# ScalarE forms two small attention operands in the first two token tiles, and small attention tiles get six buffers

## The chip, the cores and the metric

The kernel runs on one core of a Trainium2 chip. Five engines work side by side: TensorE (PE; its weight loads are PEld), VectorE (DVE), ScalarE (ACT), GpSimd (POOL) and SyncE (SP), which here only issues DMAs. The metric is the device time of one execution in microseconds, lower is better. Before the change the median of three runs is 1221.68 us (1221.15 to 1223.91).

## The reference

Three stages follow each other. Attention has 2 batches, 8 heads, 576 positions and head size 64, and keeps only the 32 largest scores of each row:

```
kth = np.partition(scores, -top_k, axis=-1)[..., -top_k:-top_k + 1]
scores = np.where(scores >= kth, scores, -1e9)
attn = np.exp(scores - np.max(scores, axis=-1, keepdims=True))
attn = attn / (np.sum(attn, axis=-1, keepdims=True) + 1e-09)
```

Its 1152 x 512 result goes through a mixture of 8 dense experts (ReLU, 512 to 1024 to 512), whose outputs are weighted by a gate that eight rounds of row and column normalisation over all tokens make. A last feed-forward layer (512 to 2048 to 512, Mish) follows.

## The kernel before, in words

The 1152 tokens form nine tiles of 128 rows, and the tiles form three chunks: tiles 0 and 1, tiles 2 and 3, tiles 4 to 8 (CHUNKS). A unit is one tile and one head (t, h). Each unit goes through five steps: scores (PE, then an eviction to SBUF by ScalarE, L235), threshold (L246 to L265), mask (L275 to L291), norm (L294 to L306) and values (transposes at L325, products with V at L348 and L355).

The threshold is VectorE's: four MAX8 instructions find eight maxima each (L254), and three MATCH_REPLACE8 strike out what was found (L261); each reads 576 columns, so a unit takes seven such passes. The first maximum, times -0.125, is the bias `nb` of the exponential (L271). The last of the 32 maxima is the threshold of the mask.

The first 13 units (POOL_UNITS; all of tile 0 and heads 0 to 4 of tile 1) are "on_pool": VectorE writes a mask of 0 or a large negative number (L285), GpSimd adds the scores (L286), and ScalarE takes the exponential and with it the row sum `sm` (L272). The other units take the exponential first and let VectorE mask and sum it (L290). In norm, `r` is the row sum plus epsilon (L299), then its reciprocal (L300), both on VectorE, and ScalarE scales the row by it (L305).

When tile 1 is done, the experts start on chunk 0. An expert is cut into eight pieces of 128 hidden columns. For a piece PE forms h (12 matmuls, L619), ScalarE rounds it to hh (L537), VectorE forms the rest hl (L538), and two pieces later PE forms y (L596). h has two PSUM buffers, so the h of piece k+2 can only start when hl of piece k has been read. The remaining attention (tiles 2 to 8) is woven between the pieces.

PE's order is written out by the program. On the other engines a scheduler sets the order, by priorities (the streams `first`, `evict`, `prep`, `attn`, `moe`, `fill`, in that order) and by when an operand would be there by its own reckoning. One rule is fixed by hand: the first MAX8 of each unit of tile 2 stands behind the last reciprocal of tile 1 (`ends`). Scores of tiles 2, 3 and parts of 5 and 6 are computed early, into tiles `early`, `early_xh`, `early_xl`.

Of the kernel before, what the change touches and what calls it, by code (L numbers as in the profile page):

```python
# [10 lines left out]
F32 = mybir.dt.float32  # L11
F32R = mybir.dt.float32r
U32 = mybir.dt.uint32
AF = mybir.ActivationFunctionType
ALU = mybir.AluOpType
# [4 lines left out]
P = 128  # L20
B, H, S, D = 2, 8, 576, 64
# [13 lines left out]
TOPK = 32  # L35
NEG = -3.0e38
SCALE = 0.125
EPS = 1e-9
TINY2 = ((1 + 1 / 16) * 2.0**-15) ** 2

CHUNKS = [(0, 1), (2, 3), (4, 5, 6, 7, 8)]
# [32 lines left out]
def attention_moe_moe2(ctx: ExitStack, tc: tile.TileContext, qT, kT, vm, vt, wg, wst, w64, out):  # L74
    nc = tc.nc
# [5 lines left out]
    def after(inst, earlier):  # L81

        tc.add_manual_dep(
            inst.ins,
            earlier.ins.name,
            mybir.DependencyInfo(mybir.DependencyClass.NoSync, mybir.DependencyReason.DATA),
            reason="order",
        )

    def pool(name, bufs=1, space=None, stack=ctx, side="left", **kw):  # L90
        if space is not None:
            kw["space"] = space
        return stack.enter_context(tc.tile_pool(name=name, bufs=bufs, side=side, **kw))

    const = pool("const")
    small = pool("small", 4)
# [13 lines left out]
    sp = pool("sp", 2, stack=att)  # L110
# [35 lines left out]
    qset, live, away = {}, {}, {}  # L146
# [98 lines left out]
    def threshold(t, h, on_pool):  # L245

        with st("attn"):
            s = live["s", t, h]
            top = small.tile([P, TOPK], F32, tag="top", name=f"top_{t}_{h}")
            w = sp.tile([P, S], F32, tag="w", name=f"w_{t}_{h}")  # L250
            src = s
            for i in range(TOPK // 8):
                g = top[:, 8 * i : 8 * i + 8]
                top8 = nc.vector.max(g, src)  # L254
                if i == 0 and t == CHUNKS[0][-1] + 1:
                    if "ends" in live:
                        after(top8, live["ends"])
                    else:
                        live.setdefault("held", []).append(top8)
                if i + 1 < TOPK // 8:  # L260
                    nc.vector.match_replace(w, g, src, NEG)  # L261
                    src = w
            live["top", t, h] = top
            if not on_pool:
                live["e", t, h] = exponential(t, h, sp.tile([P, S], F32, tag="e", name=f"e_{t}_{h}"), s, nc.vector)  # L265
        yield from ()

    def exponential(t, h, dst, src, eng, **kw):

        nb = small.tile([P, 1], F32, tag="nb", name=f"nb_{t}_{h}")  # L270
        eng.tensor_scalar(nb, live["top", t, h][:, 0:1], -SCALE, None, op0=ALU.mult)  # L271
        nc.scalar.activation(dst, src, AF.Exp, bias=nb, scale=SCALE, **kw)  # L272
        return dst

    def mask(t, h, on_pool):  # L275

        with st("attn"):
            s = live.pop(("s", t, h))
            sm = small.tile([P, 1], F32, tag="sm", name=f"sm_{t}_{h}")
            kth = live["top", t, h][:, TOPK - 1 : TOPK]  # L280
            if h % 2 == 0:
                live["pair", t, h] = sp.tile([P, 2 * S], F32, tag="em", name=f"em_{t}_{h}", bufs=3)
            em = live["pair", t, h - h % 2][:, h % 2 * S :][:, :S]
            if on_pool:
                nc.vector.tensor_scalar(em, s, kth, NEG, op0=ALU.is_lt, op1=ALU.mult)  # L285
                nc.gpsimd.tensor_tensor(em, em, s, ALU.add)  # L286
                exponential(t, h, em, em, nc.vector, accum_out=sm)
            else:
                e = live.pop(("e", t, h))
                nc.vector.scalar_tensor_tensor(em, s, kth, e, op0=ALU.is_ge, op1=ALU.mult, accum_out=sm)  # L290
            live["em", t, h], live["sm", t, h] = em, sm  # L291
        yield from ()

    def norm(t, h, on_pool):  # L294
        with st("attn"):
            em, sm = live["em", t, h], live.pop(("sm", t, h))
            r = small.tile([P, 1], F32, tag="r", name=f"r_{t}_{h}")
            with st("moe" if on_pool else "attn"):
                nc.vector.tensor_scalar(r, sm, EPS, None, op0=ALU.add)  # L299
                inv = nc.vector.reciprocal(r, r)  # L300
            if (t, h) == (CHUNKS[0][-1], H - 1):
                live["ends"] = inv
                for inst in live.pop("held", ()):
                    after(inst, inv)
            nc.scalar.activation(em, em, AF.Copy, scale=r)  # L305
        yield from ()  # L306
# [96 lines left out]
    def attention():  # L403
# [10 lines left out]
        for u, (t, h) in enumerate(units):  # L414
            pooled = u < POOL_UNITS
            for order, (stage, delay) in enumerate(
                (
                    (scores, 0),
                    (partial(threshold, on_pool=pooled), AHEAD),
                    (partial(mask, on_pool=pooled), AHEAD + 1),  # L420
                    (partial(norm, on_pool=pooled), AHEAD + (2 if pooled else 1)),
                    (values, AHEAD + (3 if pooled else 2)),
                )
            ):
                plan.setdefault(u + delay, []).append((order, u, partial(stage, t, h)))
# [434 lines left out]
```

## Time and profile before

| | |
|---|---|
| median of three runs | 1221.68 us |
| profiled execution | 1221.39 us, its span 1219.6 us |
| PE busy | 1168.7 us, 96% of the span |
| VectorE busy | 854.7 us, 70% |
| ScalarE busy | 660.2 us, 54% |
| GpSimd busy | 540.8 us, 44% |
| chain that ended last | PE 86%, DVE 11% |

Shares over the whole span hide the stages. Read them by stretch: where PE is below full there is something it waits for, and the engine that is full there sets the pace. Starts are in us from the start of the span. In a timeline the second number is the time that the row took, and an engine's next instruction can start before the last has ended; the distance from start to start is what an instruction costs its engine.

### The profile page before, as it was taken

The page shows a single profiled execution, that of the slowest core. Times are in us where ns is not written, and L with a number is a line of the kernel's source. Part 1 is how long each engine was busy: PE and PEld are TensorE (multiplying, and loading weights), DVE is VectorE, ACT ScalarE, POOL GpSimd, SP SyncE. Part 2 cuts the span into 40 slices and gives each one's busy share as a digit, 9 for nine tenths or more (in the row PEclk, how much of TensorE's full clock was granted, in tenths as well). Part 3 has the DMA queues.
Part 4 walks back from the last instruction along what each step waited for, and adds up shares of the span by engine and source line. Part 5 has one row for each costly group of instructions (what it writes and reads, how often), then busy time and mean ns, then how long its engine had stood idle before and what let it go on. Part 6 is the DMA issues. An engine that isn't in the chain of part 4 may idle for free.

```text
span 1219.6 us, 21194 instructions
## 1 busy us (share of the span) xinstructions
PE 1168.7 (96%) x7459; PEld 1048.4 (86%) x7459; DVE 854.7 (70%) x1873; ACT 660.2 (54%) x1321; POOL 540.8 (44%) x424
## 2 busy tenths in 40 slices
PE   2677999999999999999999999999999999999998
PEld 2566888998989899899999999999999999999997
DVE  7999999999999999713656868677666633433221
ACT  6786777877777778654223333333333334554432
POOL 7844778877777877774112112121121122221210
PEclk9899999999999999999999999999999999999999
DMA  8434565576655555665235665656445332223201
GB/s 258 126 129 152 171 178 170 170 224 188 211 163 168 157 162 164 186 220 169 70 89 180 199 190 176 207 178 192 138 134 160 119 98 64 93 95 114 78 26 44
DMA packets 105114, 183.20 MB, mean 150 GB/s; under 512 B 14128, under 2 KB 24624, under 8 KB 105008
## 3 DMA queue, kind: packets, MB, share of 16 engines
q1 hardware_dynamic: 103712, 180.68, 47.6%
q8 instruction: 58, 0.95, 0.3%
q10 hardware_dynamic: 1296, 1.18, 0.3%
q14 instruction: 48, 0.39, 0.1%
HBM read 158.55 MB, written 23.27 MB: 149 GB/s over the span
## 4 chain that ended last, share of the span: by engine, by line
PE 86%; DVE 11%; DMA 1%; ACT 1%; issue 0%; POOL 0%; SPq 0%; POOLq 0%; ACTq 0%
PE h_c2e L619 18%; PE y_c2e L596 18%; PE h_d L619 8%; PE y_d L596 8%; PE y_c0e L596 7%; PE h_c0e L619 7%; PE h_c1e L619 6%; PE y_c1e L596 6%; DVE top L254 4%; DVE w L261 4%; PE pv L348 2%; PE tr L325 2%; PE sc L226 2%; PE pv L355 1%; DVE em L290 1%; DMA wraw_c0e<-in_wst_dram 1%
## 5 line engine op out<-in xcount | busy, mean ns | idle before, releaser
L522 POOL TENSOR_TENSOR wl_c2e<-wraw_c2e,wh_c2e 128x512 fp32r<-128x512 f32 x64 | 84.2, 1315 | 341.2 <-ACT wh_c2e L520 326.5
L522 POOL TENSOR_TENSOR wl_c0e<-wraw_c0e,wh_c0e 128x512 fp32r<-128x512 f32 x128 | 171.6, 1356 | 53.1 <-ACT wh_c0e L520 50.9
L522 POOL TENSOR_TENSOR wl_c1e<-wraw_c1e,wh_c1e 128x512 fp32r<-128x512 f32 x128 | 173.3, 1371 | 48.6 <-ACT wh_c1e L520 45.2
L520 ACT ACTIVATE wh_c2e<-wraw_c2e 128x512 fp32r<-128x512 f32 x128 | 80.8, 632 | 186.9 <-PE y_c2e L596 95.0
L254 DVE MAX8 top<-w 128x8 f32<-128x576 f32 x216 | 157.8, 747 | 0.8
L619 PE MATMUL h_c2e<-xh,wh_c2e 128*128 128x256 f32 (+1 forms) x512 | 158.3, 309 | 0.0
L619 PE MATMUL h_c2e<-xl,wh_c2e 128*128 128x256 f32 (+1 forms) x512 | 158.0, 309 | 0.0
L619 PE MATMUL h_c2e<-xh,wl_c2e 128*128 128x256 f32 (+1 forms) x512 | 157.8, 308 | 0.0
L538 DVE SCALAR_TENSOR_TENSOR hl_c2e<-h_c2e,hh_c2e 128x256 fp32r<-128x256 f32 (+1 forms) x128 | 62.5, 488 | 99.7 <-ACT hh_c2e L537 99.3
L596 PE MATMUL y_c2e<-wh_c2e,hh_c2e 128*128 128x512 f32 x320 | 126.0, 394 | 0.0
L596 PE MATMUL y_c2e<-wl_c2e,hh_c2e 128*128 128x512 f32 x320 | 125.9, 394 | 0.0
L596 PE MATMUL y_c2e<-wh_c2e,hl_c2e 128*128 128x512 f32 x320 | 125.2, 391 | 0.0
L522 POOL TENSOR_TENSOR wl_d<-wraw_d,wh_d 128x512 fp32r<-128x512 f32 x32 | 41.5, 1297 | 160.2 <-ACT wh_d L520 160.2
L520 ACT ACTIVATE wh_c0e<-wraw_c0e 128x512 fp32r<-128x512 f32 x128 | 80.5, 629 | 52.9 <-PE y_c0e L596 21.0
L261 DVE MATCH_REPLACE8 w<-top,w 128x576 f32<-128x576 f32 x144 | 106.4, 740 | 0.0
L557 DVE TENSOR_TENSOR hl_d<-mg_d,hh_d 128x256 fp32r<-128x256 f32 x64 | 38.5, 602 | 91.7 <-ACT hh_d L556 91.7
L520 ACT ACTIVATE wh_c1e<-wraw_c1e 128x512 fp32r<-128x512 f32 x128 | 80.3, 629 | 40.4 <-PE y_c1e L596 16.4
L619 PEld LDWEIGHTS h_c2e<-xh,wh_c2e 128*128 128x128 f32 x512 | 96.2, 188 | 2.5
L619 PEld LDWEIGHTS h_c2e<-xl,wh_c2e 128*128 128x128 f32 x512 | 96.1, 188 | 2.3
L619 PEld LDWEIGHTS h_c2e<-xh,wl_c2e 128*128 128x128 f32 x512 | 96.8, 189 | 0.0
L226 PE MATMUL sc<-ks,q 128*128 128x288 f32 x320 | 63.1, 330 | 26.0 <-ACT early L239 8.2
L537 ACT ACTIVATE hh_c2e<-h_c2e 128x256 fp32r<-128x256 f32 (+1 forms) x128 | 54.8, 428 | 55.3 <-PE h_c2e L619 53.0
(170 smaller groups left out, 3352.8 us busy)
## 6 DMA issues: line engine op xcount, KB each, us to landing
wraw_c0e<-in_wst_dram SPq DMA_DIRECT2D x128, 256.0 KB, 3.0
wraw_c1e<-in_wst_dram SPq DMA_DIRECT2D x128, 256.0 KB, 3.0
wraw_c2e<-in_wst_dram SPq DMA_DIRECT2D x128, 256.0 KB, 3.0
cx<-in_w_dram SPq DMA_DIRECT2D x32, 512.0 KB, 4.2
wraw_d<-w SPq DMA_DIRECT2D x64, 256.0 KB, 2.6
yd<-ysp SPq DMA_DIRECT2D x32, 256.0 KB, 3.6
yb<-yd SPq DMA_DIRECT2D x32, 256.0 KB, 3.2
w<-cc SPq DMA_DIRECT2D x32, 256.0 KB, 3.5
```

The lines of the kernel that those rows point to most:

```text
L226: nc.tensor.matmul(halves[half], q[:, h % HG, :], ks[b, h][:, half * HS : (half + 1) * HS], start=(i == 0), stop=(i == len(terms) - 1),)
L254: top8 = nc.vector.max(g, src)
L261: nc.vector.match_replace(w, g, src, NEG)
L325: nc.tensor.transpose(tr[:, c, :], em[:, j * D + c * P :][:, :P], ident)
L348: nc.tensor.matmul(pv[i * D : (i + 1) * D, pair, c0:c1], vmain[b, pair][:, i, c, :], live["at", i][:, c, c0:c1], start=(c == 0), stop=False,)
L520: nc.scalar.activation(hi, raw, AF.Copy)
L522: eng.tensor_sub(lo, raw, hi)
L537: nc.scalar.activation(h, ps, AF.Relu)
L538: live["hl"] = nc.vector.scalar_tensor_tensor(l, ps, 0.0, h, op0=ALU.max, op1=ALU.subtract)
L557: nc.vector.tensor_sub(l, g, h)
L596: nc.tensor.matmul(y, h[:, j * P : (j + 1) * P], w, start=(f == 0 and k == 0), stop=(f == nf - 1 and k == 2),)
L619: nc.tensor.matmul(ps, w[:, c * P : (c + 1) * P], x[:, c, c0 : c0 + m], start=(k == 0), stop=(k == 3 * NC - 1),)
```

## The change

In the first two token tiles (t up to 1) `nb` is formed by ScalarE, by a copy with scale -0.125, in place of VectorE. For the 13 on_pool units ScalarE also forms `r` from the row sum, by a copy with the epsilon as bias; the reciprocal stays on VectorE. The tiles `top`, `nb` and `sm` get six buffers in place of four.

```diff
-            top = small.tile([P, TOPK], F32, tag="top", name=f"top_{t}_{h}")
+            top = small.tile([P, TOPK], F32, tag="top", name=f"top_{t}_{h}", bufs=6)
...
-    def exponential(t, h, dst, src, eng, **kw):
-        nb = small.tile([P, 1], F32, tag="nb", name=f"nb_{t}_{h}")
-        eng.tensor_scalar(nb, live["top", t, h][:, 0:1], -SCALE, None, op0=ALU.mult)
+    def exponential(t, h, dst, src, **kw):
+        nb = small.tile([P, 1], F32, tag="nb", name=f"nb_{t}_{h}", bufs=6)
+        top = live["top", t, h][:, 0:1]
+        if t <= CHUNKS[0][-1]:
+            nc.scalar.activation(nb, top, AF.Copy, scale=-SCALE)
+        else:
+            nc.vector.tensor_scalar(nb, top, -SCALE, None, op0=ALU.mult)
         nc.scalar.activation(dst, src, AF.Exp, bias=nb, scale=SCALE, **kw)
...
-            sm = small.tile([P, 1], F32, tag="sm", name=f"sm_{t}_{h}")
+            sm = small.tile([P, 1], F32, tag="sm", name=f"sm_{t}_{h}", bufs=6)
...
-                nc.vector.tensor_scalar(r, sm, EPS, None, op0=ALU.add)
+                if on_pool:
+                    nc.scalar.activation(r, sm, AF.Copy, bias=EPS)
+                else:
+                    nc.vector.tensor_scalar(r, sm, EPS, None, op0=ALU.add)
                 inv = nc.vector.reciprocal(r, r)
```

VectorE's list is 1599 rows before and 1570 now, 29 fewer; ScalarE's is 1316 and 1345. PE's order is the same. VectorE and ScalarE are also reordered, since the scheduler plans with other buffers.

First place: VectorE in tile 0, from the mask of head 0 (em_0<-s_0) to that of head 1 (em_0<-s_1). top_4 and top_5 are the maxima of heads 4 and 5, w the scores with maxima struck out. Before:

```order
20 L285 TENSOR_SCALAR em_0_227<-s_0_150,top_0_196 128x576
21 L261 MATCH_REPLACE w_2_258<-top_2_257,s_2_188 128x576
22 L271 TENSOR_SCALAR nb_3_370<-top_3_288 128x1
23 L261 MATCH_REPLACE w_1_218<-top_1_217,w_1_218 128x576
24 L254 MAX top_4_358<-s_4_249 128x8
25 L254 MAX top_2_257<-w_2_258 128x8
26 L254 MAX top_1_217<-w_1_218 128x8
27 L261 MATCH_REPLACE w_2_258<-top_2_257,w_2_258 128x576
28 L271 TENSOR_SCALAR nb_4_435<-top_4_358 128x1
29 L299 TENSOR_SCALAR r_0_272<-sm_0_226 128x1
30 L285 TENSOR_SCALAR em_0_227<-s_1_168,top_1_217 128x576
```

And now, the same stretch:

```order
17 L289 TENSOR_SCALAR em_0_227<-s_0_150,top_0_196 128x576
18 L261 MATCH_REPLACE w_2_258<-top_2_257,s_2_188 128x576
19 L254 MAX top_4_358<-s_4_249 128x8
20 L261 MATCH_REPLACE w_1_218<-top_1_217,w_1_218 128x576
21 L254 MAX top_2_257<-w_2_258 128x8
22 L254 MAX top_5_422<-s_5_286 128x8
23 L254 MAX top_1_217<-w_1_218 128x8
24 L261 MATCH_REPLACE w_2_258<-top_2_257,w_2_258 128x576
25 L307 RECIPROCAL r_0_272<-r_0_272 128x1
26 L289 TENSOR_SCALAR em_0_227<-s_1_168,top_1_217 128x576
```

Both nb and the sum with epsilon are gone, the first maxima of head 5 stand ahead of the second mask, and the reciprocal of head 0 has taken the place of its sum.

Second place: VectorE from the mask of tile 0, head 7 (em_6<-s_7) on, where the names begin again with tile 1 (em_0<-s_0 is its head 0), now:

```order
76 L289 TENSOR_SCALAR em_6_551<-s_7_420,top_7_541 128x576
77 L254 MAX top_0_603<-w_0_604 128x8
78 L307 RECIPROCAL r_6_618<-r_6_618 128x1
79 L261 MATCH_REPLACE w_0_604<-top_0_603,w_0_604 128x576
80 L254 MAX top_0_603<-w_0_604 128x8
81 L289 TENSOR_SCALAR em_0_681<-s_0_476,top_0_603 128x576
82 L254 MAX top_1_671<-s_1_539 128x8
83 L307 RECIPROCAL r_7_687<-r_7_687 128x1
84 L261 MATCH_REPLACE w_1_672<-top_1_671,s_1_539 128x576
85 L254 MAX top_1_671<-w_1_672 128x8
86 L261 MATCH_REPLACE w_1_672<-top_1_671,w_1_672 128x576
87 L307 RECIPROCAL r_0_768<-r_0_768 128x1
```

Between a mask and the reciprocal of the same head now stand six rows (head 7) and five (head 0 of tile 1). The reciprocal waits for an r that ScalarE makes. This is ScalarE there, now, with s an eviction of scores, at one of transposes and early one of the early scores:

```order
92 L276 ACTIVATE em_6_551,sm_7_612<-em_6_551,nb_7_615 128x576
93 L235 ACTIVATE s_1_539<-sc_1_534 128x576
94 L335 ACTIVATE at_4_566<-tr_4_561 128x512
95 L304 ACTIVATE r_7_687<-sm_7_612 128x1
96 L239 ACTIVATE early_xl_517<-sc_0_0_574 128x288
97 L239 ACTIVATE early_xl_517<-sc_0_1_575 128x288
98 L276 ACTIVATE em_0_681,sm_0_680<-em_0_681,nb_0_684 128x576
99 L273 ACTIVATE nb_1_765<-top_1_671 128x1
100 L312 ACTIVATE em_6_551<-em_6_551,r_7_687 128x576
101 L239 ACTIVATE early_xl_517<-sc_1_0_582 128x288
102 L304 ACTIVATE r_0_768<-sm_0_680 128x1
```

The r of a head is not right behind its exponential: two evictions stand between for head 7, and three instructions for head 0.

Third place: VectorE where the experts have begun, from hl of piece 2 to hl of piece 3 of the first expert; the other rows belong to tile 2. Before:

```order
206 L538 SCALAR_TENSOR_TENSOR hl_c0e_2_1266<-h_c0e_2_0_1267,hh_c0e_2_1265 128x256
207 L290 SCALAR_TENSOR_TENSOR em_0_1167,sm_0_1166<-early_321,top_0_1127,e_0_1136 128x576
208 L261 MATCH_REPLACE w_2_1396<-top_2_1395,early_xh_398 128x576
209 L290 SCALAR_TENSOR_TENSOR em_0_1167,sm_1_1408<-early_330,top_1_1153,e_1_1162 128x576
210 L261 MATCH_REPLACE w_3_1501<-top_3_1500,early_xh_398 128x576
211 L299 TENSOR_SCALAR r_0_1169<-sm_0_1166 128x1
212 L254 MAX top_4_1654<-early_xh_398 128x8
213 L538 SCALAR_TENSOR_TENSOR hl_c0e_3_1303<-h_c0e_3_0_1304,hh_c0e_3_1302 128x256
```

And now:

```order
186 L545 SCALAR_TENSOR_TENSOR hl_c0e_2_1266<-h_c0e_2_0_1267,hh_c0e_2_1265 128x256
187 L254 MAX top_6_1862<-early_xl_517 128x8
188 L254 MAX top_2_1395<-w_2_1396 128x8
189 L306 TENSOR_SCALAR r_1_1410<-sm_1_1408 128x1
190 L254 MAX top_7_1894<-early_xl_517 128x8
191 L254 MAX top_3_1500<-w_3_1501 128x8
192 L307 RECIPROCAL r_0_1169<-r_0_1169 128x1
193 L545 SCALAR_TENSOR_TENSOR hl_c0e_3_1303<-h_c0e_3_0_1304,hh_c0e_3_1302 128x256
```

The two masked sums em_0 of tile 2 stand ahead of hl of piece 2 now, four MAX8 that stood behind hl of piece 3 stand ahead of it, and the MAX8 of top_4 and top_5 went to the head of tile 2, with nb_4 and nb_5 soon behind.

## Rows read from the trace of the kernel before

**Rows 1.** Windows: us, busy PE, PEld, DVE, ACT, POOL (instructions), clock, DMA share, GB/s
```profile
40.00:100.00 60.00, 42.73 (x271) 34.22 (x267) 60.00 (x153) 50.05 (x117) 33.55 (x28) 0.89 0.42 135
...
122.00:180.00 58.00, 57.73 (x418) 51.26 (x420) 58.00 (x148) 42.33 (x86) 45.89 (x35) 1.00 0.58 173
180.00:510.00 330.00, 329.59 (x2471) 295.76 (x2468) 322.27 (x784) 252.10 (x491) 259.94 (x194) 1.00 0.58 179
```
**Rows 2.** Waits of PE from 122 us on: us in total, times, longest
```profile
PE h_c0e L619 <- DVE hl_c0e L538: 0.8, 1, 0.8
```
**Rows 3.** Timeline, VectorE, 21 to 33 us: start, took, instruction, idle before
```profile
21.20 0.14 DVE L271 TENSOR_SCALAR nb<-top 128x1 f32<-128x1 f32 x1
21.26 0.08 DVE L261 MATCH_VALUE_LOAD w<-top,w 128x8 f32 x1
...
21.99 0.75 DVE L254 MAX8 top<-s 128x8 f32<-128x576 f32 x1
22.66 1.40 DVE L254 MAX8 top<-w 128x8 f32<-128x576 f32 x2
...
25.62 0.15 DVE L271 TENSOR_SCALAR nb<-top 128x1 f32<-128x1 f32 x1 [0.85 <-ACT em L272]
...
32.46 0.15 DVE L271 TENSOR_SCALAR nb<-top 128x1 f32<-128x1 f32 x1 [0.36 <-ACT em L272]
```
**Rows 4.** Timeline, VectorE, 104 to 176 us
```profile
104.47 0.16 DVE L300 RECIPROCAL r<-r 128x1 f32<-128x1 f32 x1
...
121.82 0.40 DVE L538 SCALAR_TENSOR_TENSOR hl_c0e<-h_c0e,hh_c0e 128x256 fp32r<-128x256 f32 x1
...
175.73 0.41 DVE L538 SCALAR_TENSOR_TENSOR hl_c0e<-h_c0e,hh_c0e 128x256 fp32r<-128x256 f32 x1
```
**Rows 5.** Timeline, PE, 115 to 177 us: first h matmuls of pieces
```profile
115.83 0.28 PE L619 MATMUL h_c0e<-xh,wh_c0e 128*128 128x256 f32 x1
...
118.59 0.28 PE L619 MATMUL h_c0e<-xh,wh_c0e 128*128 128x256 f32 x1
...
122.27 0.39 PE L619 MATMUL h_c0e<-xh,wh_c0e 128*128 128x256 f32 x1 [0.75 <-DVE hl_c0e L538]
...
176.37 0.37 PE L619 MATMUL h_c0e<-xh,wh_c0e 128*128 128x256 f32 x1
```
**Rows 6.** Timeline, ScalarE, at 2 us
```profile
2.02 0.20 ACT L118 ACTIVATE warm<-warm 128x1 f32<-128x1 f32 x1
```
**Rows 7.** Timeline, ScalarE, 79 to 82.5 us
```profile
79.45 0.77 ACT L272 ACTIVATE em<-em,nb 128x576 f32<-128x576 f32 x1
80.11 0.20 ACT L272 ACTIVATION_READ_ACCUMULATOR em<-em,nb 128x1 f32 x1
80.21 0.77 ACT L305 ACTIVATE em<-em,r 128x576 f32<-128x576 f32 x1
80.87 0.64 ACT L235 ACTIVATE s<-sc 128x576 f32<-128x576 f32 x1
81.40 0.60 ACT L328 ACTIVATE at<-tr 128x512 f32<-128x512 f32 x1
81.88 0.72 ACT L239 ACTIVATE early<-sc 128x288 f32<-128x288 f32 x2
```
**Rows 8.** Timeline, GpSimd, at 77 us
```profile
77.48 1.42 POOL L286 TENSOR_TENSOR em<-em,s 128x576 f32<-128x576 f32 x1 [2.33 <-DVE r L299]
```
**Rows 9.** Line 285 up to 108 us: count, ns min/median/max, first and last start
```profile
L285 DVE TENSOR_SCALAR em<-s,top x13: 497/698/1721, 18.9 to 89.4; 128x576 f32<-128x576 f32 x13
```
**Rows 10.** VectorE by form, 20 to 108 us: count, busy us, mean ns, idle before
```profile
L285 DVE TENSOR_SCALAR em<-s,top 128x576 f32<-128x576 f32 x13 | 10.9, 842 | 0.0
```
**Rows 11.** Timeline, GpSimd and VectorE, at 18.8 us
```profile
18.84 1.40 POOL L158 TENSOR_TENSOR ks<-kraw,ks 64x576 fp32r<-64x576 f32 x1 [0.43 <-ACT ks L157]
...
18.91 1.65 DVE L285 TENSOR_SCALAR em<-s,top 128x576 f32<-128x576 f32 x1
```
**Rows 12.** Windows, 50 to 56.8 us, as rows 1
```profile
50.00:56.80 6.80, 3.96 (x22) 3.05 (x23) 6.80 (x20) 4.48 (x9) 4.99 (x5) 0.50 0.42 117
```

More of the change, by code (lines that the diff above doesn't have):

```diff
@@ L264, in threshold @@
             if not on_pool:
-                live["e", t, h] = exponential(t, h, sp.tile([P, S], F32, tag="e", name=f"e_{t}_{h}"), s, nc.vector)
+                live["e", t, h] = exponential(t, h, sp.tile([P, S], F32, tag="e", name=f"e_{t}_{h}"), s)
         yield from ()
-    def exponential(t, h, dst, src, eng, **kw):
-        nb = small.tile([P, 1], F32, tag="nb", name=f"nb_{t}_{h}")
-        eng.tensor_scalar(nb, live["top", t, h][:, 0:1], -SCALE, None, op0=ALU.mult)
+    def exponential(t, h, dst, src, **kw):
[5 more added lines that the diff above has]
+            nc.vector.tensor_scalar(nb, top, -SCALE, None, op0=ALU.mult)
         nc.scalar.activation(dst, src, AF.Exp, bias=nb, scale=SCALE, **kw)
@@ L286, in mask @@
                 nc.gpsimd.tensor_tensor(em, em, s, ALU.add)
-                exponential(t, h, em, em, nc.vector, accum_out=sm)
+                exponential(t, h, em, em, accum_out=sm)
             else:
```

## The prediction

> **What bounds the kernel now.** I read the windows first. In 40:100 VectorE is busy 60.00 of 60 us while PE is busy 42.73 and ScalarE 50.05; from 122 on PE is full: 57.73 of 58, then 329.59 of 330 [rows 1]. So the end is set by how early PE becomes full, since its work after that is fixed in order and amount: PE's longest wait from 122 us on is 0.8 [rows 2]. It is the last of the start: the h of piece 5 should follow at 121.35 and starts at 122.27, after an idle 0.75, when hl of piece 3 (121.82 and 0.40 of work) is written [rows 4, 5]; 121.35 is the start of piece 4's h, 118.59, and one piece of 2.76 us, as from 115.83 to 118.59 [rows 5]. Everything before stands in VectorE's queue in order, up to the last reciprocal of tile 1 at 104.47 and past it [rows 4]. The path to the end is therefore VectorE from about 20 us to 122, then PE. A microsecond saved in VectorE's queue ahead of hl of piece 3 is a microsecond of the kernel, and one added there is one lost.
>
> VectorE stays close to PE for a while: at 175.73 an hl ends at 176.14, and the h that needs its PSUM buffer starts at 176.37, a margin of 0.23 [rows 4, 5]. So what holds for piece 3 holds for the pieces up to there too.
>
> **The change part by part.** *Small instructions leave VectorE.* All 16 nb and 13 sums with epsilon go. A small one costs 0.06 from its start to the next (21.20 to 21.26) [rows 3]. The first three nb stand where VectorE waits for scores anyway and count nothing. Left are 13 nb and 13 sums: 26 x 0.06 = -1.56 us.
>
> *Two buffer waits go.* nb of heads 4 and 5 sat in VectorE's queue until the exponential four heads before had read its buffer: 0.85 at 25.62 and 0.36 at 32.46 [rows 3], in all -1.21. With six buffers and on another engine they can't stop VectorE there. Late next there is the reciprocal of head 0, which waits for ScalarE. ScalarE's new order puts that exponential ahead of the weight conversion which before waited for its DMA and held it up, so I leave the whole 1.21 as gained.
>
> *Maxima move ahead.* With six buffers the scheduler starts maxima two units earlier. By counting the third place of the change and what stands ahead of it: of what stood behind hl of piece 3 there now stand ahead of it five more MAX8 (of top_5, top_6, top_7, and a second one each of top_2 and top_3), two nb, one sum and one reciprocal. A MAX8 costs 0.67 from start to start (21.99 to 22.66) [rows 3]: 5 x 0.67 + 4 x 0.06 = +3.59. This is no extra work, it is only done sooner, and VectorE is ahead by it later. But PE can't use that: it needs hl. The same count gives +3.6 for hl of piece 0 (three MAX8, two MATCH_REPLACE at 0.73 by 21.26 to 21.99 [rows 3], two nb). For hl of piece 2, which also gets the two masked sums ahead of it, the count is higher, but the wait of PE came one piece later, so there was room. PE's own pace, 2.76 a piece, doesn't cover it, since h of piece 5 had only 0.92 of stall behind it, which I count once: the new order costs 3.59 less the 0.05 between the end of hl and the start of h, +3.54.
>
> *Small instructions come to ScalarE.* 29 of them. The nearest rows for a 128x1 there are the warm-up, 0.20 [rows 6], and the read of the accumulator, which costs 0.10 from start to start (80.11 to 80.21) [rows 7]: 2.9 to 5.8 us of ScalarE's time, of which about 22 fall in 40:100, where it has 10 us free [rows 1]. ScalarE works in order, so its idle time is not all usable: it waits for PE, for GpSimd and for VectorE's reciprocals. The Trainium skill (ScalarE: Activation LUTs, Rules for kernel authors) says to put additions and multiplications on VectorE, not ScalarE, and its section on table loads gives 186 ns for an instruction with immediate scale and bias before its columns, of which about 93 overlap. The trace agrees, with 0.20 and 0.10 [rows 6, 7]; by the page the 29 would take an estimated 2.7 us. Its rule would have the change lose, which is the first rival below.
>
> *A new wait.* Before, VectorE waited on nothing for r: the sum with epsilon stood in its queue well after the exponential. Now the reciprocal waits for mask, GpSimd, exponential and r in turn. The second place of the change shows the two tightest. From the mask of head 7 to its reciprocal VectorE has three MAX8, one MATCH_REPLACE, one small one and one mask: 3 x 0.67 + 0.73 + 0.06 + 0.43 = 3.2 (a mask undisturbed is 0.50 [rows 9], less 0.07 that it shares with its neighbour). The way round takes 1.42 on GpSimd [rows 8], 0.76 for the exponential with its accumulator (79.45 to 80.21), an eviction s 0.53 (80.87 to 81.40) and at 0.48 (81.40 to 81.88) [rows 7], r 0.20 [rows 6], and about 0.2 for the handovers: 3.6, a wait of 0.4. For head 0 of tile 1 there are 2.9 us of VectorE and 0.4 of the wait before, 3.3 together, against 1.42 + 0.76 + 0.10 for an nb + 0.66 for a row scaled (80.21 to 80.87) + 0.29 for half of the two early evictions [rows 7] + 0.20 + 0.2 = 3.6: a wait of 0.3. The other eleven have at least four us of VectorE between; for them, and for scores that ScalarE evicts later because of the new work, I add 0.6. Together +1.3. What is queued behind the waiting reciprocal is the next MAX8 and so the whole path. Bounds: 0, if ScalarE's free time covers it all, and 4.4, if all 22 of the stretch 40:100 lie on the path at 0.20 each. I take 1.3, nearer to the lower end, because two waits can be worked out and the rest have room.
>
> *Masks that meet GpSimd.* A mask takes 0.50 alone and up to 1.72 [rows 9]; 13 of them 13 x 0.842 = 10.95 in all [rows 10], 4.45 more than 13 x 0.50. The one at 18.91 took 1.65, ending after GpSimd's instruction of 18.84 to 20.24 [rows 11]. The Trainium skill (SBUF — State Buffer, Who interferes with whom) says why: such a VectorE instruction and GpSimd's share a pair of ports, and the one that starts first keeps it for its whole length. Which masks meet GpSimd is dealt anew by the new order. I take no change; it may be 2.2 us either way, half of the 4.45.
>
> **Sum.** -1.56 - 1.21 + 3.54 + 1.3 = +2.07 on the profiled execution of 1221.39 (span 1219.6 and 1.8 around it): 1223.4. It stands 0.3 under the median of 1221.68, so against that the change is +1.7 us, 0.14%. A measurement of this kernel tells 0.2%, 2.4 us, from no change: faster is under 1219.2, slower over 1224.1.
>
> **Rivals.** *ScalarE paces the start, slower.* In 40:100 it is busy 50 of 60 us [rows 1] and now also the link between a row sum and its reciprocal; each r waits for the accumulator just written. The place is tile 0's last heads and tile 1's first, and the price is the upper bound of the wait, 4.4 in place of 1.3: 1226.5. It decides from a wait of 2.0 us in all, where the sum passes 1224.1. For it speaks that two of 13 waits are already 0.7, against it that ScalarE has 10 us free.
>
> *The moved maxima cost nothing, faster.* If PE is not held by hl there, for instance because GpSimd's or ScalarE's side of the weights is what is late, or if fewer masks meet GpSimd, the 2.77 saved stays: 1218.6. Against it speaks that PE names VectorE's hl as what it waited for at 122.27 [rows 5], and that hl and h stay within 0.23 at 176 [rows 4, 5].
>
> *The saving just covers the order, no change.* With no new wait the sum is +0.77: 1222.2. This is the forecast's own lower side.
>
> *PE's clock.* In 50:56.8 the granted clock was 0.50, the 1.2 GHz level, after PE had stood idle a good part of the time before [rows 12]; it hurt nothing since VectorE was the bound. Should such a spell fall behind 108 us, where PE is nearly full, 6.8 us of work at half pace add 3.4: 1226.8. Against it: 1.00 in the windows from 122 on [rows 1].
>
> **How the numbers follow.** Forecast, a wait between 0 and 2.0: 0.57. ScalarE paces: 0.31. Clock: 0.05. Moved maxima free or masks luckier: 0.07. Slower is 0.31 + 0.05 = 0.36, same 0.57, faster 0.07. The low end of the range is the sum with no new wait and the masks 2.2 better, 1219.9, a little lower for the case with free maxima: 1219.6. The high end is the upper bound of the wait: 1226.5.
>
> **What would show it.** Right: VectorE has no nb wait at 25 us; its last reciprocal of tile 1 comes 1 to 2.5 us before 104.47; reciprocals of the on_pool units show idle time behind ScalarE's r, about 1.3 in all; the last xl and hl of piece 0 come later after that reciprocal by 3.6; PE's first full piece starts at about 124.3 and the rest follows unchanged. Wrong: PE full before 121 us (the order costs nothing), or the last reciprocal later than 104.5 (ScalarE paces), or a difference that arises behind 180 us.

## The result

The changed kernel takes 1232.74 us (median of 4 runs, 1231.4 to 1235.9) against 1222.8 before (4 runs): 1.0085 times as long, 95% interval 1.006 to 1.011. Forecast were 1223.4 and a range up to 1226.5: the sign of the likeliest sum was right, the size was not. The profiled execution took 1233.08, its span 1231.2 (before 1219.6), 11.7 us more than the one of before, the medians 9.9 more.

The windows of after (us, busy PE, PEld, DVE, ACT, POOL, clock, DMA share, GB/s) answer to [rows 1], its list of waits of PE from 122 us on to [rows 2]:

```profile
40.00:100.00 60.00, 42.66 (x268) 33.88 (x265) 59.41 (x132) 50.59 (x134) 33.60 (x28) 0.86 0.42 133
122.00:180.00 58.00, 58.00 (x411) 51.18 (x409) 58.00 (x145) 42.42 (x84) 44.62 (x36) 1.00 0.58 176
180.00:510.00 330.00, 328.46 (x2437) 293.29 (x2436) 320.26 (x768) 248.73 (x485) 252.00 (x192) 1.00 0.58 177
```

```profile
PE tr L332 <- ACT at L335: 1.5, 2, 1.3
```

By these views little has changed: PE is full from 122 us on at a clock of 1.00, and the list there has 1.5 us of waits (two, the longer 1.3). But the counts fall: 418 matmuls in 122:180 before, 411 now, 2471 and 2437 in 180:510, in the same order. After starts some 3 us later, so the two windows do not hold quite the same work, and the counts only hint that a busy PE got less done.

The timeline of VectorE, after (start, took, instruction, idle before):

```profile
26.34 0.16 DVE L307 RECIPROCAL r<-r 128x1 f32<-128x1 f32 x1 [0.70 <-ACT r L304]
...
104.55 0.16 DVE L307 RECIPROCAL r<-r 128x1 f32<-128x1 f32 x1
...
109.37 0.28 DVE L370 TENSOR_TENSOR xl<-pv,xh 128x128 fp32r<-128x128 f32 x1
114.04 0.27 DVE L370 TENSOR_TENSOR xl<-pv,xh 128x128 fp32r<-128x128 f32 x1
116.34 0.41 DVE L545 SCALAR_TENSOR_TENSOR hl_c0e<-h_c0e,hh_c0e 128x256 fp32r<-128x256 f32 x1
...
124.85 0.40 DVE L545 SCALAR_TENSOR_TENSOR hl_c0e<-h_c0e,hh_c0e 128x256 fp32r<-128x256 f32 x1
```

The two waits of [rows 3] for a buffer of nb are gone; a wait for ScalarE's r stands at 26.34. The last reciprocal of tile 1 (104.47 in [rows 4]) is at 104.55, hl of piece 0 (112.51 before) at 116.34, hl of piece 3 (121.82 in [rows 4]) at 124.85. PE's piece 5 starts at 125.36, where [rows 5] have 122.27.

Since PE runs the same instructions in the same order, starts of equal pieces can be subtracted, and this shows where the rest went. Pieces are counted from 0 through all eight experts of a chunk (0 to 63); c0, c1, c2 are the chunks and d is the last layer. The table has the start of piece 5 of c0 and five stretches from the start of one piece to that of a later one (us), each from two rows of PE's timeline:

| kernel | piece 5 | c0 5 to 63 | c0 63 to c1 9 | c1 9 to 62 | c2 4 to 62 | c2 62 to d 10 |
|---|---|---|---|---|---|---|
| before | 122.27 | 211.52 | 34.13 | 185.63 | 407.15 | 72.24 |
| after | 125.36 | 213.54 | 36.05 | 187.10 | 409.33 | 73.09 |
| difference | 3.09 | 2.02 | 1.92 | 1.47 | 2.18 | 0.85 |

With 0.4 between c1 62 and c2 4 this makes 11.9 us: 3.1 are the start that was forecast as 2.07, 1.5 the two waits, and some 7.3 are lost bit by bit. A piece without attention (a plain piece), PE's timeline, before and then after (first h, first y, next h):

```profile
542.51 0.28 PE L619 MATMUL h_c1e<-xh,wh_c1e 128*128 128x256 f32 x1
543.90 0.39 PE L596 MATMUL y_c1e<-wh_c1e,hh_c1e 128*128 128x512 f32 x1
545.27 0.28 PE L619 MATMUL h_c1e<-xh,wh_c1e 128*128 128x256 f32 x1
```

```profile
550.79 0.28 PE L626 MATMUL h_c1e<-xh,wh_c1e 128*128 128x256 f32 x1
552.21 0.39 PE L603 MATMUL y_c1e<-wh_c1e,hh_c1e 128*128 128x512 f32 x1
553.61 0.28 PE L626 MATMUL h_c1e<-xh,wh_c1e 128*128 128x256 f32 x1
```

h takes 1.42 in place of 1.39, y 1.40 in place of 1.37, the piece 2.82 in place of 2.76 (2.81 in the pieces around it). Each row says "0.28" or "0.39" in both kernels: what a matmul takes is not what it costs, the distance from start to start is. Nothing waits here, and the clock is 1.00 in both.

### The profile page after: what moved, and what is told of

It reads as the page before. It is cut to its first block, busy times and chain, and to the rows that moved or that the text cites. A ratio compares the mean times of both kernels' runs of the same rounds, so it can differ in the third digit from the quotient of the medians.

```text
span 1231.2 us, 21182 instructions
## 1 busy us (share of the span) xinstructions
PE 1178.0 (96%) x7459; PEld 1051.5 (85%) x7459; DVE 858.4 (70%) x1844; ACT 661.5 (54%) x1350; POOL 533.5 (43%) x424
## 4 chain that ended last, share of the span: by engine, by line
PE 89%; DVE 7%; DMA 1%; ACT 1%; issue 0%; POOL 0%; SPq 0%; ACTq 0%; POOLq 0%
PE y_c2e L603 18%; PE h_c2e L626 18%; PE h_d L626 8%; PE y_d L603 8%; PE y_c1e L603 7%; PE h_c0e L626 7%; PE h_c1e L626 7%; PE y_c0e L603 7%; DVE top L254 3%; DVE w L261 3%; PE pv L355 2%; PE tr L332 2%; PE sc L226 2%; PE pv L362 1%; DVE em L289 1%; DMA kraw<-in_kT_dram 1%
## 5 line engine op out<-in xcount | busy, mean ns | idle before, releaser
L529 POOL TENSOR_TENSOR wl_c0e<-wraw_c0e,wh_c0e 128x512 fp32r<-128x512 f32 x128 | 169.0, 1331 | 59.9 <-ACT wh_c0e L527 54.0
L529 POOL TENSOR_TENSOR wl_c1e<-wraw_c1e,wh_c1e 128x512 fp32r<-128x512 f32 x128 | 169.8, 1343 | 56.7 <-ACT wh_c1e L527 56.1
```

Source lines behind the costliest of these rows:

```text
L529: eng.tensor_sub(lo, raw, hi)
```

## The experiments

Two things differ for PE's operands: what the other engines do beside it, and where the tiles lie. Two more buffers each of top (128 bytes a partition), nb and sm (32 each) are 384 bytes; every tile allocated after the pool small on the left side moves up by that, the experts' inputs and hh and hl among them, while their weights, on the right side, stay. Each time below comes with its ratio to runs of the kernel before on the same chip and the 95% interval.

**The shift alone, and the change without it.** a_shift384 has every instruction of before, in its order:

```diff
     small = pool("small", 4)
+    pool("shift").tile([P, 96], F32, name="shift")
```

> The kernel before with one unused tile of 384 bytes a partition behind the pool small; every instruction stands as before on every engine, and all tiles allocated after small on the left side (the inputs of the experts, hh and hl among them) lie 384 bytes higher, as the six buffers put them, while the experts' weights on the right side stay. Theory 1 (addresses): the profile of after shows a plain piece of the experts at 2.81 us where before has 2.76, with the same matmuls, and this grows to about 7.4 us by the end (11.97 late at the last piece, less 3.1 at piece 5 and 1.5 of one wait); if where the operands lie does this, the time is 1222.8 + 7.4 = 1230.2 and a plain piece 2.81. Theory 2 (what the other engines do beside PE in the new order slows the matmuls): 1222.8, within 0.2%, and a plain piece of 2.76.

Measured: 1229.81, 1.0071 (1.0059 to 1.0083). In its timeline a plain piece takes 2.81:

```profile
545.71 0.28 PE L620 MATMUL h_c1e<-xh,wh_c1e 128*128 128x256 f32 x1
547.12 0.39 PE L597 MATMUL y_c1e<-wh_c1e,hh_c1e 128*128 128x512 f32 x1
548.52 0.28 PE L620 MATMUL h_c1e<-xh,wh_c1e 128*128 128x256 f32 x1
```

Its stretches are those of after (213.59, 187.10, 409.32, 73.09), but for c0 63 to c1 9, which takes 34.55: a has no such wait. An unused tile costs 0.7%, most of what the change costs.

b_after_at_before has the instructions of after, in its order, at the addresses of before:

```diff
     small = pool("small", 4)
+    pool("hold").tile([P, 192], F32, name="hold")
...
     hp = pool("hp", LAG + 1, stack=att)
+    late = pool("late", 4, stack=att)
...
-            top = small.tile([P, TOPK], F32, tag="top", name=f"top_{t}_{h}", bufs=6)
+            top = late.tile([P, TOPK], F32, tag="top", name=f"top_{t}_{h}", bufs=6)
```

(nb and sm alike.)

> The changed kernel, every instruction as there, but top, nb and sm with their six buffers lie in a pool of their own behind all others on the left side, and an unused tile fills their old place, so that all other tiles but r lie as before. Theory 1 (addresses): what is left is the late start and one wait, 3.1 + 1.5 us, and the time is 1232.7 - 7.4 = 1225.3, a plain piece 2.76. Theory 2 (order): 1232.7 as the changed kernel, a plain piece 2.81.

Measured: 1224.69, 1.0029 (1.0017 to 1.004); piece 5 at 124.88, then 212.51, 35.75, 185.17, 407.15 and 72.24. Theory 1 holds both ways: the shift makes the slow pieces, the new order as it stands in b doesn't.

**How far, and against what.** More shifts of the kernel before; only the size of the tile differs from a_shift384.

> The kernel before with 128 unused bytes behind the pool small in place of the 384 of a_shift384 (which cost 9.4 us, a plain piece of 2.81 for 2.76). Theory 1 (it is the place of left against right that counts, with some period): a piece anywhere from 2.74 to 2.81, 1219 to 1230, and another one than with 512. Theory 2 (any shift away from the present place costs the same): 2.81, 1229.8.

> The kernel before with 512 unused bytes behind the pool small. Theory 1 with a period of 512 or a divisor of it: a plain piece of 2.76 as before, 1220.5; with a longer period, or by theory 2 (any shift costs): 2.78 to 2.81, 1224 to 1230.

> The kernel before with 256 unused bytes behind the pool small. Theory 1 with a period of 256: a plain piece of 2.76 and 1222 as before; with a period of 512: slower, 2.78 to 2.81 and 1226 to 1230, or faster than before, under 2.76, if before stands at no best place.

> The kernel before with 64 unused bytes behind the pool small, the first shift that is no multiple of 128. Theory 1: the place at which left and right operands stand to each other decides, and 64 may lie on either side, a plain piece from 2.70 to 2.81, 1215 to 1230. Rival (what counts is only whether left operands begin at certain multiples, as 0 and 512 do): 2.81 or more, 1229 or more.

> The kernel before with 192 unused bytes behind the pool small. With a period of 256, 192 stands as far on one side of the present place as 64 on the other; a piece from 2.70 to 2.81, 1215 to 1230. Rival (only multiples of 256 or 512 are good): 2.81 or more, 1229 or more.

| shift, bytes | median, us | ratio (interval) | a plain piece of chunk 1: h + y | c2 4 to 62 |
|---|---|---|---|---|
| 64 | 1228.93 | 1.0067 (1.0053 to 1.008) | 1.43 + 1.39 | 407.32 |
| 128 | 1229.03 | 1.0051 (1.0033 to 1.007) | 1.41 + 1.40 | 409.33 |
| 192 | 1234.28 | 1.011 (1.0095 to 1.0126) | 1.43 to 1.44 + 1.38 to 1.40 | 411.25 |
| 256 | 1220.71 | 0.9995 (0.9985 to 1.0005) | 1.39 + 1.37 | 404.11 |
| 512 | 1221.89 | 0.9999 (0.9985 to 1.0012) | 1.39 + 1.37 | 404.08 |

Multiples of 256 are free; the others cost 6 to 13 us. 128 and 384 differ by 256, and their last chunks agree to 0.01 (409.33 and 409.32). The last column has two levels where nothing or a multiple of 256 is added: 407.15 in before and b, some 404.1 here (see the end). The rival of g_shift64 and g_shift192 (only such multiples are good) is what came out. h_after_512 uses that: after, unaltered but for 128 unused bytes, which fill its 384 up to 512.

```diff
     small = pool("small", 4)
+    pool("shift").tile([P, 32], F32, name="shift")
```

> The changed kernel, unaltered but for 128 unused bytes a partition behind the pool small, so that with the 384 of its six buffers the left side lies 512 higher than before. A shift of 512 alone left the kernel before at its time and at 2.76 a plain piece, 128 and 384 cost 7 to 9 us. Theory 1 (the place modulo 512 or less counts): the changed kernel comes down from 1232.7 to 1225, 0.2 to 0.4% over before, its late start alone being left, a plain piece 2.76. Theory 2 (what six buffers do costs by itself): 1229 or more, 2.81.

Measured: 1224.38, 1.0026 (1.0015 to 1.0037), as b_after_at_before. l_after_right128 leaves the left side of after where it is and lowers the weights:

```diff
-    pool("edge", side="right").tile([P, 8], F32, name="edge")
+    pool("edge", side="right").tile([P, 40], F32, name="edge")
```

> The changed kernel with the unused tile at the far right edge 128 bytes larger, so that all weights on the right lie 128 lower while the left lies 384 higher: against each other 512, two periods. Theory 1 (the place of left against right): 1224.5 as without the shift, a plain piece 2.76. Theory 2 (each side's own place): 1232.7, or another slow value, 2.81.

Measured: 1222.62, 1.0007 (0.9995 to 1.002). Its plain piece is back at 2.76, with every left tile still 384 higher than before:

```profile
547.11 0.28 PE L626 MATMUL h_c1e<-xh,wh_c1e 128*128 128x256 f32 x1
548.49 0.39 PE L603 MATMUL y_c1e<-wh_c1e,hh_c1e 128*128 128x512 f32 x1
549.87 0.28 PE L626 MATMUL h_c1e<-xh,wh_c1e 128*128 128x256 f32 x1
```

So it is the place of one side against the other that counts, and by the shifts above it counts modulo 256 bytes. The median is under that of h_after_512 though l starts as late (piece 5 at 125.29). In the profiles the last chunk, c2 4 to 62, took 403.98 in l, 405.16 in h and 407.15 in b (see the end); whether that makes the medians differ was not tested.

Which operand? In h the inputs stream and the weights are loaded, in y the weights stream and hh or hl is loaded. f_hp_shift384 puts a tile of 384 bytes ahead of hp alone; k_x_shift384 moves the inputs by 384 and hp by 512:

```diff
     small = pool("small", 4)
+    pool("shift").tile([P, 96], F32, name="shift")
...
+    pool("shift2", stack=att).tile([P, 32], F32, name="shift2")
     hp = pool("hp", LAG + 1, stack=att)
```

> The kernel before with 384 unused bytes a partition ahead of the pool hp, so that hh and hl alone lie 384 bytes higher, every instruction as before. Theory 1 (a matmul slows where its two operands stand to each other as the shift puts them): only y, which reads hh and hl, slows, 1.40 a piece in place of 1.37, and h stays at 1.39: 128 pieces x 0.03 = 3.8, 1224.3. Theory 2 (something that all matmuls share, not the operands' own places): h slows too, or neither.

> The kernel before with 384 unused bytes behind the pool small and 128 more ahead of hp: the inputs of the experts (xh, xl) lie 384 higher as in the changed kernel, hh and hl of the first two chunks 512 higher, which is a whole period. Theory (operand by operand, the counterpart of f_hp_shift384, where y alone slowed to 1.40): h slows to 1.41 in the first two chunks and y stays at 1.37; in the last chunk both slow as in a_shift384, since hp2 is moved by 384 there. 1226 to 1228. Rival (the place of hh and hl is what counts): 1.39 and 1.37, 1222.

Measured: f 1221.76, 0.9993 (0.998 to 1.0006); k 1226.92, 1.0039 (1.0025 to 1.0053). In the plain pieces of chunk 1, f has y at 1.39 to 1.40 in every piece and h at 1.38 and 1.42 by turns; k has h at 1.41 to 1.42 in every piece and y at 1.37 and 1.39 by turns. Half of the theory holds: the part whose left operand was moved is slow each time, but the other one slows in every second piece too. f's cost was forecast as 3.8 and is not seen in its time: its stretches are 212.54 and 185.79 in the first two chunks, 1.2 more than before, and 407.14 in the last, where it moves nothing. What meets there is open.

The Trainium skill (SBUF — State Buffer, Who interferes with whom) says that PE never waits on anyone, and (TensorE: Matmul & The Clock Gate, Step-by-step: what each phase is for) that loading the next weights takes no read bandwidth from the running matmul, since PE has two ports. Neither section speaks of where the operands lie; taken alone they would leave a shift without cost. The runs differ, 0.7% for 384 bytes, so the measurement decides; which of PE's two reads is held up, no run here shows.

**The late start.** Two runs split the change, both at the addresses of before. c_six_only is b_after_at_before with nb and the sum with epsilon on VectorE again; d_scalar_four is after without the three `bufs=6`.

> Only the six buffers of top, nb and sm, with nb and the sum with epsilon on VectorE as before, and the other tiles (but r) at the addresses of before. Theory 1 (addresses for the drift, moved maxima for the late start): the two buffer waits, 1.21 us, are gone and hl of the first pieces comes some 3.6 us later behind the last reciprocal of tile 1: 1222.8 + 2.4 = 1225.2, a plain piece 2.76. Theory 2 (the new order slows the matmuls too): 1230 or more. If the late start is ScalarE's doing and not that of the moved maxima: 1221.6.

> Only the move of nb and of the sum with epsilon to ScalarE; four buffers, and so all addresses, as before. Theory 1: VectorE saves 1.55 us of small instructions and loses about 0.9 to waits for r and 0.6 to a later third score, the maxima of tile 2 don't move ahead: 1222.8, within 0.2%, a plain piece 2.76. Rival (the way over ScalarE is what makes the start late, 3 to 4 us): 1226 to 1227.

Measured: c 1219.93, 0.9991 (0.998 to 1.0001); d 1221.59, 1.0009 (0.9998 to 1.0019). c refutes its forecast: six buffers alone don't make the start late. The plain piece of 2.76 is missed in part too. c has the addresses of before, and yet its pieces change pace at piece 57 of c1, the second row here (first h of pieces 56, 57, 58 and 59):

```profile
537.59 0.28 PE L622 MATMUL h_c1e<-xh,wh_c1e 128*128 128x256 f32 x1
540.35 0.29 PE L622 MATMUL h_c1e<-xh,wh_c1e 128*128 128x256 f32 x1
543.16 0.28 PE L622 MATMUL h_c1e<-xh,wh_c1e 128*128 128x256 f32 x1
545.97 0.28 PE L622 MATMUL h_c1e<-xh,wh_c1e 128*128 128x256 f32 x1
```

From 2.76 it goes to 2.81 and stays there to piece 62, with no wait of PE. So the slow pace can come without a shift as well; what starts it there is open.

Now the start. From the last reciprocal of tile 1 to hl of piece 0 (the first and the last row) VectorE takes 8.29 us in c and 11.79 in b_after_at_before. c first, then b:

```profile
104.16 0.16 DVE L303 RECIPROCAL r<-r 128x1 f32<-128x1 f32 x1
106.22 0.27 DVE L366 TENSOR_TENSOR xl<-pv,xh 128x128 fp32r<-128x128 f32 x1
110.14 0.28 DVE L366 TENSOR_TENSOR xl<-pv,xh 128x128 fp32r<-128x128 f32 x1
112.45 0.41 DVE L541 SCALAR_TENSOR_TENSOR hl_c0e<-h_c0e,hh_c0e 128x256 fp32r<-128x256 f32 x1
```

```profile
103.89 0.16 DVE L309 RECIPROCAL r<-r 128x1 f32<-128x1 f32 x1
108.71 0.28 DVE L372 TENSOR_TENSOR xl<-pv,xh 128x128 fp32r<-128x128 f32 x1
113.38 0.27 DVE L372 TENSOR_TENSOR xl<-pv,xh 128x128 fp32r<-128x128 f32 x1
115.68 0.41 DVE L547 SCALAR_TENSOR_TENSOR hl_c0e<-h_c0e,hh_c0e 128x256 fp32r<-128x256 f32 x1
```

It is 8.04 to 8.05 in before, in d_scalar_four and in all runs with the order of before, and 11.79 in the four with the order of after (after, b, h, l). In the orders 11 passes over 576 columns stand between the two in before, c and d, and 16 in after; ahead of the xl of the third pair of tile 1 (the first xl above) 3 in c and 7 in after. Only with both parts does the scheduler put six first maxima ahead of that xl. e_xl_first tests this on b_after_at_before, with one more fixed rule:

```diff
+                if i == 0 and t == CHUNKS[0][-1] + 1 and h >= 4:
+                    if "lastxl" in live:
+                        after(top8, live["lastxl"])
+                    else:
+                        live.setdefault("held4", []).append(top8)
...
-                    nc.vector.tensor_sub(lo, pv[:, pair, :], hi)
+                    lx = nc.vector.tensor_sub(lo, pv[:, pair, :], hi)
+                if h == H - 1:
+                    live["lastxl"] = lx
+                    for held in live.pop("held4", ()):
+                        after(held, lx)
```

> The changed kernel at the addresses of before (as the run b_after_at_before, 1224.7), with one more fixed rule: the first MAX8 of heads 4 to 7 of tile 2 stands behind the last xl of tile 1. Between the last reciprocal of tile 1 and hl of piece 0 VectorE then has 12 passes over 576 columns in place of 16, and the last xl stands behind 8 of them in place of 11. Theory (the late start is that of the maxima that moved ahead of xl and hl): hl of piece 0 comes some 3 us earlier after that reciprocal, piece 5 starts 2.6 us earlier than in b_after_at_before, and the time is 1222.1. Rival (PE or ScalarE is late there anyway): 1224.7 and the same start.

Measured: 1222.5, 1.0000 (0.9986 to 1.0014); hl of piece 0 comes 9.68 after the reciprocal, 2.1 earlier than in b_after_at_before. Forecast were some 3, but the timeline has 13 passes there, not the 12 of the forecast, and three fewer at 0.67 are 2.0. Piece 5 starts at 121.72, 3.2 earlier, as this profile's reciprocal was early too (102.27). So the start was late by the passes ahead of xl and hl. PE's timeline of after shows it from the other side: PE waits 2.96 for an xl and then 0.53 for hl of piece 0.

```profile
109.79 1.98 PE L355 MATMUL pv<-at,vm 128*64 128x128 f32 x16 [2.96 <-DVE xl L370]
116.81 0.39 PE L626 MATMUL h_c0e<-xh,wh_c0e 128*128 128x256 f32 x1 [0.53 <-DVE hl_c0e L545]
```

i_scalar_first_tiles and j_vector_first_tiles give six buffers to tiles 0 and 1 alone, from a pool of their own behind hp (j with VectorE's nb and sum):

```diff
+    six = pool("six", 6, stack=att)
...
+    def few(t):
+        return six if t <= CHUNKS[0][-1] else small
...
-            top = small.tile([P, TOPK], F32, tag="top", name=f"top_{t}_{h}", bufs=6)
+            top = few(t).tile([P, TOPK], F32, tag="top", name=f"top_{t}_{h}")
```

(nb and sm alike.)

> The changed kernel at the addresses of before, with six buffers for top, nb and sm of the first two tiles alone; the later tiles have four. Between the last reciprocal of tile 1 and hl of piece 0 stand 13 passes over 576 columns on VectorE (before 11, the changed kernel 16), to hl of piece 3 23 (21 and 26). Theory (the maxima of tile 2 that six buffers let go ahead make the start late): two passes more in place of five, 1.3 us in place of 3.75, against which the small instructions and buffer waits saved stand: 1222 to 1223, some 2 us under the 1224.5 of the changed kernel without its shift. Rival (ScalarE's new link makes the start late): 1224.5.

> Only six buffers for top, nb and sm of the first two tiles, nothing on ScalarE, addresses of before. VectorE has as many passes ahead of hl as before (11, 13, 16, 21), and the two waits for a buffer of nb (0.85 and 0.36) are gone. Theory: 1.2 us faster than before, 1220.5 against 1221.7, about what a measurement can tell. Rival (another wait takes the place of the two): the time of before.

Measured: i 1223.17, 1.0006 (0.9994 to 1.0018), with 13 passes and 9.62 from the reciprocal to hl, as its theory had it; j 1221.39, 0.9991 (0.998 to 1.0003). In j waits of 1.6 for a row sum and 1.3 for scores stand where [rows 3] had 1.21 for nb: the rival, or a gain too small to tell. No version beats the kernel before beyond its interval; c and j, both without ScalarE's part, come nearest.

## Why the prediction was wrong, step by step

**The step that failed** is the first: "So the end is set by how early PE becomes full, since its work after that is fixed in order and amount." Order and amount are fixed, the pace is not. The list of signs had "a difference that arises behind 180 us" as one that would refute it, and it did: some 7.3 of 11.9 us arise along all pieces (a plain piece 2.81 to 2.82 in place of 2.76), and the same 384 bytes alone cost 0.71%. The 7.3 are on the low side: the profile of before ran its last chunk at the slower of two paces (see the end), 407.15, and beside the 404.1 of others at multiples of 256 after loses 5.2 there, not 2.2. Six buffers were costed by what they let the scheduler do, not by the bytes that they take. With the shift made harmless the change costs 0.29% (b), 0.26% (h) and 0.07% (l, no difference clear of noise), 3.5, 3.2 and 0.9 us, inside the range.

**Maxima move ahead.** +3.54 forecast, by hl of piece 3. Behind the reciprocal it came 17.35 to 17.42 us in the profiles with the order of before and 20.30 to 20.54 in the four with that of after, 2.9 to 3.2 later; hl of piece 0, counted as +3.6, came 3.75 later. Piece 5 starts 0.05 to 0.10 behind the end of hl of piece 3 in all four. So the mechanism was right and the size near, the attribution to six buffers alone was not.

**The last reciprocal of tile 1.** Forecast was -1.56 - 1.21 + 1.3 = -1.47. Over the profiles with each order it stands at 104.40 before (nine, 103.11 to 105.36) and 104.16 after (four, 103.89 to 104.55): -0.24, within the spread. For the same reason the 104.55 of after, which by the list of signs would speak for ScalarE (later than 104.5), shows nothing. The terms, from the same profiles:
- Small instructions: forecast 1.56, measured 1.56 by the distances from start to start (13 nb 0.80, 13 sums 0.76).
- Buffer waits of nb: 1.0 to 3.0 in the nine, mean 1.6; all gone.
- Waits for r: forecast 1.3, measured 0.6 to 2.0, mean 1.0. They lie elsewhere: at head 0 of tile 0 (0.70 at 26.34), where the prediction left the whole saving as gained, and hardly at the two places that it worked out (none and 0.19, forecast 0.4 and 0.3). No row stands behind the 0.2 for handovers in those two sums, nor behind the 0.6 added for the rest, so the total is near by luck.
- Not forecast: VectorE's waits for scores, in the mean 3.4 before, all ahead of 20 us, and 4.35 after, of which 3.3 lie there; the rest stands in two of the four profiles, at about 23 us and once at 73. Why was not tested.
- Not forecast: passes of one head that stand back to back, though the second place of the change shows them (rows 79 to 81). After, the same three in the timeline of VectorE:

```profile
61.10 0.74 DVE L261 MATCH_REPLACE8 w<-top,w 128x576 f32<-128x576 f32 x1
61.88 0.76 DVE L254 MAX8 top<-w 128x8 f32<-128x576 f32 x1
62.75 0.63 DVE L289 TENSOR_SCALAR em<-s,top 128x576 f32<-128x576 f32 x1
```

The MAX8 reads what the MATCH_REPLACE8 wrote and starts 0.78 after it, and the mask that needs the MAX8 0.87 after that; either distance is 0.66 to 0.67 elsewhere, as in [rows 3]. From 20 us to the last reciprocal there is one such pair in before and there are seven in after, each 0.12 to 0.20 longer: 0.8 us for the six.

Together these make -1.56 - 1.6 + 1.0 + 0.95 + 0.8 = -0.4, against the -0.24 of the means.

**Piece 5.** Forecast 124.3; measured 124.9 to 125.4. **Masks:** 13 x 0.853 = 11.1 after, 10.95 before; over the profiles 9.0 to 11.1 after (mean 10.1) and 9.1 to 11.0 before (mean 10.2), no change as taken. **The wait for "at" ahead of "tr"** (1.3 at 354) was not forecast; but four of the nine profiles with the order of before have 35.8 to 35.9 us in that stretch too (36.05 in after), so it can't be laid to the change.

**Rivals.** None explains the result. ScalarE's busy time in 40:100 rose by 0.54 and it paces nothing. The clock rival's condition did come: in the profile of after the granted clock was at its lower level, 1.2 GHz, once more behind 108 us, after PE had stood idle for the 2.96 above (0.51 in this window; the columns are those of [rows 1]).

```profile
109.30:112.60 3.30, 2.81 (x20) 2.51 (x21) 3.30 (x14) 1.62 (x3) 0.00 (x0) 0.51 0.02 5
```

b, h and l have such a spell too, at about 108.4 to 115.6. Its price did not come: in all four piece 2 starts 0.05 to 0.06 behind the end of hl of piece 0, and VectorE has no idle time between the last reciprocal and that hl, so VectorE sets the start there.

## What to carry to other kernels

A buffer more is also a shift of everything allocated after it: where PE is full, measure a change of buffers beside the same kernel with an unused tile of that size, and, as long as it measures as it did here, fill pools up to a multiple of 256 bytes a partition. Compare a full engine by the distance from start to start of equal work, for its busy share and the times of single rows don't show a slower pace. Two edits that do nothing each can reorder a scheduler's program together; count what stands ahead of the instruction that the critical engine waits for.

## What was not expected of the hardware

- A plain piece takes 2.76 us where the left operands lie at the place of before against the right ones, or 256 or 512 bytes from it, and 2.81 to 2.84 at 64, 128, 192 and 384, with the clock at 1.00. No profile at the latter four shows 2.76. But at the place of before 2.81 occurs too, in the last plain pieces of c (540.35 to 543.16), so the place is not all that counts.
- An instruction of VectorE that reads what the pass just ahead of it wrote starts 0.78 to 0.87 us behind it (61.10, 61.88, 62.75 above), where 0.66 to 0.67 is the rule in these timelines. That it is the reading that delays it was not tested by a run of its own.
- In the last chunk a piece takes 6.97 or 6.90 us at the same clock. Before ran at 6.97 (755.02 to 761.99) until late in the chunk; g_shift256, with the same instructions, at 6.90 (753.82 to 760.72). That is 3 us between profiles (407.15 and 404.1), while the times of before spread over 4 to 9 us on one chip. h_after_512 changes over within the chunk, from 6.90 (805.98 to 812.88) to 6.97 (819.92 to 826.89). What decides it is open. No profile at a shift of 64, 128, 192 or 384 shows 6.90 in these plain pieces; they take 6.96, 6.99, 7.03 and 6.99.
